# Transposing x, B and C by DMA while loading, in a kernel of two sequence mixers (convolution and complex state space)

## The chip, the cores and the metric

The kernel runs on one core of one Trainium2 chip. The metric is the device time of one execution in microseconds (us).

## The reference

The inputs are bf16 with sequence length S = 2048 and width D = 1024. Two independent halves are computed and laid side by side in the output of 1 x 2048 x 2048.

Half A: a causal convolution of length 4 on k, a product with v, a causal long convolution by a filter of length S, and a gate by q.

```python
k_shift = sum(k_pad[:, t:t + S, :] * shift_k[:, ks - 1 - t] for t in range(4))
kv = k_shift * v
y = irfft(rfft(kv, 2*S) * rfft(ssm_k, 2*S))[:S] + kv * ssm_D
a = q * y
```

Half B: a diagonal complex recurrence with 1024 states.

```python
Lam_bar = exp(dt * Lam)
B_bar = ((Lam_bar - 1.0) / Lam)[:, None] * (B_re + 1j * B_im)
Bu = einsum("bld,pd->blp", x, B_bar)
h[t] = Lam_bar * h[t-1] + Bu[t]
b = 2.0 * einsum("blp,dp->bld", h, C_re + 1j * C_im).real + x * Dskip
```

## The kernel before

Everything is emitted into one function, `full_kernel`; a framework then gives each engine its own instruction queue. It may move an instruction that has its inputs ready ahead of earlier ones that have not, and puts in the waits. The engines are TensorE (PE, its weight loads shown as PEld), VectorE (DVE), ScalarE (ACT), GpSimd (POOL) and SyncE (SP). Loads from device memory are issued on SP's queue by `dma` (L84), stores and some moves on POOL's by `dmas_` (L87). Each queue is in order.

Half B cuts time into 16 chunks of 128 steps (index i) and the states into 8 groups of 128 (index j). TensorE contracts over partitions, so it needs x, B and C with the contracted dimension on partitions, that is transposed from how they lie in memory.

- `b_load_x` (L248) loads a chunk of x of 128 x 1024 into `xn` (three buffers). `b_xT` (L253) transposes it by eight 128 x 128 TensorE transposes against `ident` into a PSUM tile `pt` and copies that to `xT` (seven buffers), on ACT, for chunk 0 on DVE.
- `bt_prep` (L596) does the same for the 16 blocks of B (j = 0..7, real and imaginary), through `bn` (three buffers) into `BT`; the real blocks are copied by DVE, the imaginary by ACT.
- `ct_load` (L609) and `ct_prep` (L614) do the same for the 16 blocks of C, through `bn` into `CT`, copied by ACT. The imaginary blocks are multiplied by -1 in that copy.
- `b_u` (L265) multiplies `BT` with `xT`, eight matmuls of 128 x 128 for each (i, j, c), and ACT copies the result to `u` (five buffers).
- `b_rot_ops` (L283) is the recurrence on DVE: 14 steps a chunk. It rotates `u` by the tables `ci` and `si`, runs two scans of 128 x 1024, and multiplies by the tables `eor` and `eoi` to give `h`.
- `b_y` (L337) multiplies `h` with `CT`, adds the skip term (`xT` with the diagonal matrices `Dd`), and the result goes out as `yo`.
- `gen_tables_a` and `gen_tables_b` (L216, L229) make the tables in the setup, on DVE and ACT. Their scratch arrays `sc_*` lie in the memory of `CT`, so `CT` can be written only when the tables are done. `params_rest` (L163) makes the small coefficients for them.

Half A is a Fourier transform split in two steps. Stage A1 makes 16 rows of kv on DVE from `krow` (six buffers) and `vt` (three buffers), eight ops each (`a1_kv_ops`, L397). It transforms them and the filter by matmuls (L427, L474) and stores them to device memory (`Ys_kv`, `Ys_h`). Stage A2 has 32 groups: load `l2k`, `l2h` and weights, matmuls (L508), a swap of the partition halves of `ha` into `hb` by DMA, two products on DVE (L519, L521), matmuls (L532, L533), store to `Vs`. Stage A3 has 16 rows: load `vv` and `qt`, matmuls, a product, store.

The order is written by hand as ticks: `at(t, kind, fn)` puts a step at tick t, and the main loop runs the ticks, with each tick's TensorE steps of A and B interleaved, then its DVE steps. Chunk i of the recurrence takes ticks 8i to 8i+7 and its `b_y` the eight after. `b_u` runs ahead at a rate of 1.5 groups a tick to tick 40 and 0.7 after, as far as the `u` buffers allow (`u_tick`). The part that concerns the change:

```python
tu = u_tick[(i, 0)]
at(tu - 12, "misc", lambda i=i: b_load_x(i))
at(tu - 2, "pe_b", lambda i=i: b_xT(i))
...
at(n // 2 - 1, "misc", lambda c=c, dd=dd: ct_load(c, dd))
at(n // 2, "pe_b", lambda c=c, dd=dd: ct_prep(c, dd, "s"))
```

Before the ticks a setup runs: x of chunk 0, `gen_tables_a`, the 16 `bt_prep` with `b_u` of chunk 0 one group behind them, `params_rest`, `gen_tables_b`, and the first loads of half A.

Of the kernel before, what the change touches and what calls it, by code (L numbers as in the profile page):

```python
# [13 lines left out]
ALU = mybir.AluOpType  # L14
F32 = mybir.dt.float32
BF16 = mybir.dt.bfloat16
# [45 lines left out]
def full_kernel(ctx, tc, A_q, A_k, A_v, A_shift_k, A_ssm_k, A_ssm_D, B_x, B_Lre, B_Lim, B_Bre, B_Bim,  # L62
                B_Cre, B_Cim, B_log_dt, B_Dskip, out, cfg=None):
    cfg = dict(cfg or {})
    nc = tc.nc
    P = 128
    S, D = A_q.shape[-2], A_q.shape[-1]
    L = S
    NP = B_Lre.shape[0]
    NJ = NP // P  # L70
    ND = D // P
    T = 128
# [5 lines left out]
    q, k, v, x = A_q[0], A_k[0], A_v[0], B_x[0]  # L78
# [5 lines left out]
    def dma(out_, in_):  # L84
        return nc.sync.dma_start(out_, in_)
# [6 lines left out]
    ps_t = ctx.enter_context(tc.tile_pool(name="ps_t", bufs=2, space=PSUM))  # L92
# [136 lines left out]
    def gen_tables_b():  # L229
        nc.vector.tensor_copy(ci[:], sc_vc)  # L230
        nc.vector.tensor_copy(si[:], sc_vs)
        for j in range(NJ):
            nc.scalar.activation(sc_rn[:, j, :], sc_vc[:, j, :], ACT.Copy, scale=br2[:, j:j + 1])
            nc.scalar.activation(sc_ang[:, j, :], sc_vs[:, j, :], ACT.Copy, scale=br2[:, j:j + 1])
        for j in range(NJ):
            nc.vector.scalar_tensor_tensor(eor[:, j, :], sc_vs[:, j, :], nbi2[:, j:j + 1], sc_rn[:, j, :], ALU.mult, ALU.add)
            nc.vector.scalar_tensor_tensor(eoi[:, j, :], sc_vc[:, j, :], bi2[:, j:j + 1], sc_ang[:, j, :], ALU.mult, ALU.add)
# [6 lines left out]
    state = {}  # L244
# [1 line left out]
    XT_BUFS = U_BUFS + 2  # L246

    def b_load_x(i):  # L248
        xn = xpool.tile([P, D], BF16, name="xn", bufs=3)
        dma(xn[:], x[i * T:(i + 1) * T, :])  # L250
        state[("xn", i)] = xn

    def b_xT(i, eng="s"):  # L253
        xn = state.pop(("xn", i))
        xT = xpool.tile([P, ND, T], BF16, name="xT", bufs=XT_BUFS)
        state[("xT", i)] = xT
        pt = ps_t.tile([P, ND, P], BF16, name="pt")
        for dd in range(ND):
            nc.tensor.transpose(pt[:, dd, :], xn[:, dd * P:(dd + 1) * P], ident[:])
        if eng == "v":  # L260
            nc.vector.tensor_copy(xT[:], pt[:])
        else:
            nc.scalar.copy(xT[:], pt[:])  # L263

    def b_u(i, j, c):  # L265
        xT = state[("xT", i)]
# [16 lines left out]
    def b_rot_ops(i):  # L283
        ops = []
# [304 lines left out]
        for o in ops:  # L589
            o()  # L590

    bnpool = ctx.enter_context(tc.tile_pool(name="bn", bufs=1))
    Bv = (B_Bre.rearrange("(j i) d -> i j d", i=P), B_Bim.rearrange("(j i) d -> i j d", i=P))
    Cv = (B_Cre, B_Cim)

    def bt_prep(j, c, eng):  # L596
        bn = bnpool.tile([P, D], BF16, name="bn", bufs=3)
        dma(bn[:], Bv[c][:, j, :])
        pt = ps_t.tile([P, ND, P], BF16, name="pt")
        for dd in range(ND):  # L600
            nc.tensor.transpose(pt[:, dd, :], bn[:, dd * P:(dd + 1) * P], ident[:])  # L601
        if eng == "v":
            nc.vector.tensor_copy(BT[:, j, c, :, :], pt[:])
        else:
            nc.scalar.copy(BT[:, j, c, :, :], pt[:])

    cnat = {}

    def ct_load(c, dd):  # L609
        cn_ = bnpool.tile([P, NP], BF16, name="bn", bufs=3)  # L610
        dma(cn_[:], Cv[c][dd * P:(dd + 1) * P, :])
        cnat[(c, dd)] = cn_

    def ct_prep(c, dd, eng):  # L614
        cn_ = cnat.pop((c, dd))
        pt = ps_t.tile([P, NJ, P], BF16, name="pt")
        for j in range(NJ):
            nc.tensor.transpose(pt[:, j, :], cn_[:, j * P:(j + 1) * P], ident[:])
        dst = CT[:, :, c, dd * P:(dd + 1) * P]
        if c == 0:  # L620
            if eng == "v":
                nc.vector.tensor_copy(dst, pt[:])
            else:
                nc.scalar.copy(dst, pt[:])
        else:
            if eng == "v":
                nc.vector.tensor_scalar(dst, pt[:], -1.0, None, ALU.mult)
            else:
                nc.scalar.mul(dst, pt[:], -1.0)

    NT = 8 * (NCH + 1) + 8
    ev = {}
# [34 lines left out]
    if DO_B:  # L667
        for i in range(NCH):
            t0 = 8 * i
            rops = {}  # L670
            at(t0, "misc", lambda i=i, rops=rops: rops.update({"l": b_rot_ops(i)}))
            for kk, sl in enumerate([[0, 1], [2, 3], [4, 5], [6], [7], [8, 9], [10, 11], [12, 13]]):
                for oi in sl:
                    at(t0 + kk, "dve_b", lambda oi=oi, rops=rops: rops["l"][oi]())
            for kk in range(8):
                at(t0 + 8 + kk, "pe_b", lambda i=i, kk=kk: b_y(i, kk // 4, kk % 4))
            if i >= U_PRO:
                tu = u_tick[(i, 0)]
# [74 lines left out]
    if DO_B:  # L753
        for i in range(U_PRO):
            b_load_x(i)
        gen_tables_a()
        b_xT(0, "v")
        for j in range(NJ):
            bt_prep(j, 0, "v")
            bt_prep(j, 1, "s")  # L760
            if j >= 1:
                b_u(0, j - 1, 0)
                b_u(0, j - 1, 1)
            if j == 1:
                params_rest()
        b_u(0, NJ - 1, 0)
        b_u(0, NJ - 1, 1)
        for i in range(1, U_PRO):
            b_xT(i)
            for j in range(NJ):  # L770
                for c in range(2):
                    b_u(i, j, c)
# [72 lines left out]
```

## Time and profile before

| what | value |
|---|---|
| median of 3 runs | 431.73 us (428.91 to 433.8) |
| profiled execution, first to last instruction | 431.1 us; the page gives no time outside it |
| PE busy | 380.7 us, 88% of the span |
| DVE busy | 350.7 us, 81% |
| ACT busy | 303.6 us, 70% |
| POOL busy | 130.2 us, 30% |
| SP's DMA queue | 58.60 MB, 42.7% of 16 engines' span |
| POOL's DMA queue | 43.01 MB, 28.8% |
| mean granted TensorE clock | 0.974 |

Matmuls are pipelined and their records overlap, so a busy PE is not PE at its peak, and the shares are averages over stages with different limits. In the slices each digit is the busy share of a fortieth of the span in tenths. In the groups a row is one source line on one engine, with its count, its busy time, the mean duration of one, and the idle time of the engine just before with what ended it. In the chain each step goes back to what released it.

### The profile page before, as it was taken

Reading aid. Unit: us, or ns where it says so; the run is one execution under the profiler, and the core shown is the slowest. Engines: PE = TensorE matmul, PEld = TensorE weight load, DVE = VectorE, ACT = ScalarE, POOL = GpSimd, SP = SyncE. Lnnn points to the kernel's source line nnn. Section 1 sums busy time; section 2 is a strip of 40 time slices with the busy share of each in tenths; the row PEclk is TensorE's granted clock in tenths of the full one; section 3 lists DMA queues with packets and bytes.
Section 4 is the critical chain, followed back from the end, with each engine's and each line's share of the span. In section 5 each row is a group of like instructions: output and inputs, shape, how many; then the busy total and the mean of one; then the engine's idle time right before and its main releaser. Section 6 shows DMA issues by size and latency. Waiting matters only on the chain.

```text
span 431.1 us, 9757 instructions
## 1 busy us (share of the span) xinstructions
PE 380.7 (88%) x3713; PEld 259.7 (60%) x3713; DVE 350.7 (81%) x642; ACT 303.6 (70%) x531; POOL 130.2 (30%) x224
## 2 busy tenths in 40 slices
PE   2589799797987997999899999999899999997784
PEld 2578687575765875775556566566465666763331
DVE  2989999999999999936897979797959637976830
ACT  1977999787886887646678877878568783344451
POOL 4000344464654455311222232322122211012121
PEclk9979999999999899999999999999899999999989
DMA  7879987778776544397778687879666523959981
GB/s 247 285 255 309 336 289 254 265 240 249 276 235 205 167 163 159 120 334 238 229 241 263 217 247 245 265 234 295 195 217 181 165 69 135 298 176 396 403 316 73
DMA packets 41353, 102.23 MB, mean 237 GB/s; under 512 B 6621, under 2 KB 8925, under 8 KB 41306
## 3 DMA queue, kind: packets, MB, share of 16 engines
q1 hardware_dynamic: 27322, 58.60, 42.7%
q0 software_dynamic: 13984, 43.01, 28.8%
q8 instruction: 29, 0.48, 0.5%
q14 instruction: 18, 0.15, 0.1%
HBM read 59.64 MB, written 33.55 MB: 216 GB/s over the span
## 4 chain that ended last, share of the span: by engine, by line
PE 42%; DVE 28%; issue 12%; DMA 10%; ACT 5%; POOL 2%; SPq 0%; POOLq 0%; DVEq 0%; ACTq 0%
PE pu L274 13%; PE py L345 13%; DVE m L409 5%; PE psa L508 5%; DVE acc L410 4%; DMA hb<-ha 3%; PE psa L533 3%; PE psa L532 3%; DVE ta L305 2%; DVE tb L308 2%; DVE acc L414 2%; DMA out_dram<-ot 2%; POOL out_dram L88 2%; DMA bn<-in_B_C_re_dram 1%; PE pt L601 1%
## 5 line engine op out<-in xcount | busy, mean ns | idle before, releaser
L274 PE MATMUL pu<-xT,BT 128*128 128x128 bf16 x2048 | 156.1, 222 | 0.5 <-ACT xT L263 0.3
L274 PEld LDWEIGHTS <-BT 128*128 128x128 bf16 x2048 | 136.2, 100 | 33.5 <-issue 2.4
L345 PE MATMUL py<-CT,h 128*128 128x512 bf16 x512 | 140.2, 382 | 2.3 <-ACT yo L355 2.3
L345 PEld LDWEIGHTS <-h 128*128 128x128 bf16 x512 | 46.7, 98 | 45.5 <-issue 4.9
L88 POOL DMA_DIRECT2D hb<-ha x64 | 33.4, 526 | 88.9 <-ACT ha L509 85.0
L534 ACT CAST vsb<-psa 128x512 bf16<-128x512 f32 x64 | 37.0, 602 | 25.7 <-PE psa L533 24.8
L88 POOL DMA_DIRECT2D Ys_h<-ysbh x64 | 45.6, 716 | 30.8 <-ACT ysbh L475 29.4
L277 ACT CAST u<-pu 128x512 bf16<-128x512 f32 x64 | 39.4, 615 | 13.2 <-PE pu L274 13.1
L428 ACT CAST ysb<-psa 128x512 bf16<-128x512 f32 x64 | 38.5, 644 | 13.7 <-PE psa L427 13.3
L519 DVE TENSOR_TENSOR ha<-x,ha 128x1024 bf16<-128x1024 bf16 x32 | 21.9, 684 | 27.8 <-DMA hb<-ha 18.7
L475 ACT CAST ysbh<-psa 128x512 bf16<-128x512 f32 x64 | 38.7, 641 | 5.5 <-issue 2.3
L509 ACT CAST ha<-psa 128x512 bf16<-128x512 f32 x64 | 36.8, 598 | 7.3 <-PE psa L508 6.3
L509 ACT CAST x<-psa 128x512 bf16<-128x512 f32 x64 | 36.9, 593 | 7.3 <-PE psa L508 5.2
L308 DVE TENSOR_TENSOR_SCAN tb<-rtab,tb 128x1024 bf16<-128x1024 f32 x16 | 36.6, 2285 | 0.0
L305 DVE TENSOR_TENSOR_SCAN ta<-rtab,ta 128x1024 bf16<-128x1024 f32 x16 | 36.5, 2280 | 0.0
L427 PE MATMUL psa<-acc,F1t 128*128 128x512 bf16 x64 | 24.6, 392 | 12.0 <-DVE acc L414 11.9
L564 ACT CAST ot<-psa 128x512 bf16<-128x512 f32 x32 | 17.9, 589 | 24.4 <-DMA out_dram<-ot 14.8
L409 DVE TENSOR_TENSOR m<-krow,wbc 128x1024 bf16<-128x1024 bf16 x48 | 32.4, 675 | 0.0
L410 DVE TENSOR_TENSOR acc<-acc,m 128x1024 bf16<-128x1024 bf16 x48 | 32.3, 673 | 0.0
L532 PE MATMUL psa<-ha,wts 128*128 128x512 bf16 x64 | 24.5, 384 | 4.2 <-DVE ha L519 4.0
L88 POOL DMA_DIRECT2D Ys_kv<-ysb x32 | 17.8, 557 | 33.9 <-ACT ysb L428 33.9
L350 PE MATMUL py<-Dd,xT 128*128 128x128 bf16 x128 | 28.0, 219 | 0.0
(139 smaller groups left out, 628.5 us busy)
## 6 DMA issues: line engine op xcount, KB each, us to landing
Ys_kv<-ysb POOLq DMA_DIRECT2D x32, 256.0 KB, 2.9
Ys_h<-ysbh POOLq DMA_DIRECT2D x64, 128.0 KB, 3.3
l2k<-Ys_kv SPq DMA_DIRECT2D x16, 512.0 KB, 6.0
l2h<-Ys_h SPq DMA_DIRECT2D x16, 512.0 KB, 4.2
hb<-ha POOLq DMA_DIRECT2D x64, 128.0 KB, 3.7
Vs<-vsb POOLq DMA_DIRECT2D x16, 512.0 KB, 5.9
vv<-Vs SPq DMA_DIRECT2D x32, 256.0 KB, 6.6
xn<-in_B_x_dram SPq DMA_DIRECT2D x16, 256.0 KB, 4.3
```

The lines of the kernel that those rows point to most:

```text
L88: return nc.gpsimd.dma_start(out_, in_)
L274: nc.tensor.matmul(pu[:, c, jl, :], BT[:, j, c, dd, :], xT[:, dd, :], start=(dd == 0), stop=(dd == ND - 1))
L277: nc.scalar.copy(u[:, :, j - 1:j + 1, :], pu[:])
L305: ops.append(lambda: nc.vector.tensor_tensor_scan(fl(st["ta"]), fl(rtab), fl(st["ta"]), 0.0, ALU.mult, ALU.add))
L308: nc.vector.tensor_tensor_scan(fl(st["tb"]), fl(rtab), fl(st["tb"]), 0.0, ALU.mult, ALU.add)
L345: nc.tensor.matmul(py[:], h[:, c, j, :], CT[:, j, c, dh * 512:(dh + 1) * 512], start=(j == 0 and c == 0), stop=(j == NJ - 1 and c == 1))
L409: ops.append(lambda jj=jj: nc.vector.tensor_mul(st["m"][:], krows[n2 - jj][:], wbc[:, jj, :]))
L410: ops.append(lambda: nc.vector.tensor_add(st["acc"][:], st["acc"][:], st["m"][:]))
L428: nc.scalar.copy(ysb[:, dh * 512:(dh + 1) * 512], pt[:])
L475: nc.scalar.copy(ysbh[:, :, n2l, :], pt[:].rearrange("p (c d) -> p c d", c=2))
L509: nc.scalar.copy(d_[:, dh * 512:(dh + 1) * 512], pt[:])
L532: nc.tensor.matmul(pt[:], wts[:, gi, 1, :], ha[:, dh * 512:(dh + 1) * 512], start=True, stop=False)
```

## The change

x, B and C are transposed by the DMA itself, by `dma_start_transpose` on SP's queue, straight from device memory into `xT`, `BT` and `CT`. The TensorE transposes, the PSUM tiles and the copies of these three go, and with them `xn` and `bn`. The transposes of the filter in half A (`a1h_T`) stay. A chunk of x and a block of B is one DMA of 128 x 1024; C is four DMAs of 512 x 1024. The 16 loads of B are emitted ahead of `gen_tables_a`, the four of C after `gen_tables_b`.

[...]the -1 of C's imaginary part moves: `eoi` is made with the opposite sign, the step that used it for the real part of `h` changes from subtract to add, and the one for the imaginary part from add to subtract, so that the imaginary part of `h` comes out negated.

```diff
         for j in range(NJ):
             nc.vector.scalar_tensor_tensor(eor[:, j, :], sc_vs[:, j, :], nbi2[:, j:j + 1], sc_rn[:, j, :], ALU.mult, ALU.add)
-            nc.vector.scalar_tensor_tensor(eoi[:, j, :], sc_vc[:, j, :], bi2[:, j:j + 1], sc_ang[:, j, :], ALU.mult, ALU.add)
+            nc.vector.scalar_tensor_tensor(eoi[:, j, :], sc_vc[:, j, :], nbi2[:, j:j + 1], sc_ang[:, j, :], ALU.mult, ALU.subtract)
...
     def b_load_x(i):
-        xn = xpool.tile([P, D], BF16, name="xn", bufs=3)
-        dma(xn[:], x[i * T:(i + 1) * T, :])
-        state[("xn", i)] = xn
-
-    def b_xT(i, eng="s"):
-        xn = state.pop(("xn", i))
         xT = xpool.tile([P, ND, T], BF16, name="xT", bufs=XT_BUFS)
+        nc.sync.dma_start_transpose(xT[:], x[i * T:(i + 1) * T, :])
         state[("xT", i)] = xT
-        pt = ps_t.tile([P, ND, P], BF16, name="pt")
-        for dd in range(ND):
-            nc.tensor.transpose(pt[:, dd, :], xn[:, dd * P:(dd + 1) * P], ident[:])
...
-        ops.append(lambda: nc.vector.tensor_sub(st["h"][:, 0, :, :], st["h"][:, 0, :, :], st["u"][:, 1, :, :]))
+        ops.append(lambda: nc.vector.tensor_add(st["h"][:, 0, :, :], st["h"][:, 0, :, :], st["u"][:, 1, :, :]))
...
-            nc.vector.tensor_add(st["h"][:, 1, :, :], st["h"][:, 1, :, :], st["u"][:, 1, :, :])
+            nc.vector.tensor_sub(st["h"][:, 1, :, :], st["h"][:, 1, :, :], st["u"][:, 1, :, :])
...
-    def bt_prep(j, c, eng):
...
-    def ct_prep(c, dd, eng):
...
+    def bt_load(j, c):
+        nc.sync.dma_start_transpose(BT[:, j, c, :, :], Bv[c][:, j, :])
+
+    def ct_load(c, hf):
+        nc.sync.dma_start_transpose(CT[:, :, c, hf * 512:(hf + 1) * 512], Cv[c][hf * 512:(hf + 1) * 512, :])
...
                 at(tu - 12, "misc", lambda i=i: b_load_x(i))
-                at(tu - 2, "pe_b", lambda i=i: b_xT(i))
...
-        for n, (c, dd) in enumerate([(c, dd) for dd in range(ND) for c in range(2)]):
-            at(n // 2 - 1, "misc", lambda c=c, dd=dd: ct_load(c, dd))
-            at(n // 2, "pe_b", lambda c=c, dd=dd: ct_prep(c, dd, "s"))
...
         for i in range(U_PRO):
             b_load_x(i)
+        for j in range(NJ):
+            for c in range(2):
+                bt_load(j, c)
         gen_tables_a()
-        b_xT(0, "v")
         for j in range(NJ):
-            bt_prep(j, 0, "v")
-            bt_prep(j, 1, "s")
-            if j >= 1:
-                b_u(0, j - 1, 0)
-                b_u(0, j - 1, 1)
-            if j == 1:
+            b_u(0, j, 0)
+            b_u(0, j, 1)
+            if j == 0:
                 params_rest()
...
         gen_tables_b()
+        for hf in range(2):
+            for c in range(2):
+                ct_load(c, hf)
```

More of the change, by code (lines that the diff above doesn't have):

```diff
@@ L248, in b_load_x @@
     def b_load_x(i):
-        xn = xpool.tile([P, D], BF16, name="xn", bufs=3)
-        dma(xn[:], x[i * T:(i + 1) * T, :])
-        state[("xn", i)] = xn
-    def b_xT(i, eng="s"):
-        xn = state.pop(("xn", i))
         xT = xpool.tile([P, ND, T], BF16, name="xT", bufs=XT_BUFS)
+        nc.sync.dma_start_transpose(xT[:], x[i * T:(i + 1) * T, :])
         state[("xT", i)] = xT
-        pt = ps_t.tile([P, ND, P], BF16, name="pt")
-        for dd in range(ND):
[L259 to L263, printed above, removed]
     def b_u(i, j, c):
@@ L590, in run @@
             o()
-    bnpool = ctx.enter_context(tc.tile_pool(name="bn", bufs=1))
     Bv = (B_Bre.rearrange("(j i) d -> i j d", i=P), B_Bim.rearrange("(j i) d -> i j d", i=P))
     Cv = (B_Cre, B_Cim)
-    def bt_prep(j, c, eng):
[L597 to L612, printed above, removed]
-    def ct_prep(c, dd, eng):
[L615 to L629, printed above, removed]
+    def bt_load(j, c):
+        nc.sync.dma_start_transpose(BT[:, j, c, :, :], Bv[c][:, j, :])
+    def ct_load(c, hf):
+        nc.sync.dma_start_transpose(CT[:, :, c, hf * 512:(hf + 1) * 512], Cv[c][hf * 512:(hf + 1) * 512, :])
     NT = 8 * (NCH + 1) + 8
@@ L755, in full_kernel @@
             b_load_x(i)
+        for j in range(NJ):
+            for c in range(2):
+                bt_load(j, c)
         gen_tables_a()
-        b_xT(0, "v")
         for j in range(NJ):
-            bt_prep(j, 0, "v")
-            bt_prep(j, 1, "s")
-            if j >= 1:
-                b_u(0, j - 1, 0)
-                b_u(0, j - 1, 1)
-            if j == 1:
-                params_rest()
[L766 to L772, printed above, removed]
+            b_u(0, j, 0)
+            b_u(0, j, 1)
+            if j == 0:
+                params_rest()
         gen_tables_b()
+        for hf in range(2):
+            for c in range(2):
+                ct_load(c, hf)
     if DO_A:
```

## Prediction

> **What bounds the kernel now.** I read the page's slices first, then the table by windows, the timeline where the setup ends, and the chain of work that ended last. The slices (each digit a tenth of 10.8 us) show that the bound changes:
>
> ```profile
> PE   2589799797987997999899999999899999997784
> ...
> DVE  2989999999999999936897979797959637976830
> ...
> PEclk9979999999999899999999999999899999999989
> DMA  7879987778776544397778687879666523959981
> ```
>
> VectorE (DVE) is full from slice 2 to slice 16, TensorE (PE) from slice 17 to slice 35, and at the end neither is. The windows put sizes to it (window, length, then busy us of PE, weight loads, DVE, ACT, POOL, granted clock, DMA share, GB/s):
>
> ```profile
> 36.00:48.00 12.00, 10.13 (x159) 8.93 (x157) 11.96 (x18) 10.15 (x15) 1.08 (x2) 1.00 0.98 342
> 60.00:80.00 20.00, 19.37 (x228) 15.09 (x226) 20.00 (x36) 20.00 (x33) 9.81 (x15) 1.00 0.84 274
> 240.00:280.00 40.00, 39.65 (x331) 23.81 (x330) 34.72 (x61) 32.25 (x60) 11.96 (x23) 1.00 0.79 254
> 320.00:360.00 40.00, 39.89 (x358) 25.04 (x356) 24.80 (x42) 30.40 (x56) 10.70 (x20) 1.00 0.49 148
> 385.00:432.00 47.00, 33.25 (x171) 14.78 (x169) 21.16 (x30) 17.14 (x32) 9.77 (x18) 0.94 0.77 292
> ```
>
> Three stages. From 11 to 172 us DVE sets the pace: 11.96 of 12 and 20.00 of 20 us, with PE waiting on its products. From about 178 to 385 us PE does: 39.65 and 39.89 of 40 us. After 385 us the last section waits on vv loads, ACT copies and output stores; the change has nothing there. The last column but one is the warning: between 36 and 80 us the DMA engines are already 84 to 98% busy.
>
> The seam between setup and stage one, on DVE (start, length):
>
> ```profile
> 32.19 0.69 DVE L406 TENSOR_TENSOR acc<-krow,wbc 128x1024 bf16<-128x1024 bf16 x1
> ...
> 33.92 0.68 DVE L603 COPY BT<-pt 128x1024 bf16<-128x1024 bf16 x1
> 34.52 0.34 DVE L237 SCALAR_TENSOR_TENSOR eoi<-CT,bi 128x128 bf16<-128x128 f32 x1
> ...
> 37.31 0.68 DVE L292 TENSOR_TENSOR ta<-u,ci 128x1024 bf16<-128x1024 bf16 x1
> ```
>
> Here the convolution's first product starts at 32.19, the last BT copy on DVE is at 33.92, the last table op ends at 34.8, and the first rotation op (L292) at 37.31 follows ACT's last BT copy (34.58) and the last u copy (36.31). Two convolution ops of 0.6 us lie before 34.8, so setup holds DVE until an effective 33.6 us.
>
> **What is removed, as the groups price it** (busy, mean ns | idle before):
>
> ```profile
> L263 ACT COPY xT<-pt 128x1024 bf16<-128x1024 bf16 x15 | 15.9, 1060 | 1.7 <-PE pt L259 1.7
> ...
> L601 PE MATMUL pt<-ident,bn 128*128 128x128 bf16 x128 | 12.4, 258 | 6.4 <-ACT BT L605 3.6 <-DMA bn<-in_B_B_im_dram 1.9 <-DVE BT L603 0.6
> ...
> L603 DVE COPY BT<-pt 128x1024 bf16<-128x1024 bf16 x8 | 5.5, 687 | 2.1 <-PE pt L601 2.0
> ```
>
> Records of pipelined matmuls overlap, so 219 ns is not the price. On the chain eight transposes count 0.45 us, that is 56 ns each:
>
> ```profile
> 262.81 0.45 PE pt L259 x8
> ```
>
> **What the Trainium skill says.** "DMA: Bandwidth & Descriptors", section "Latency and other measured facts", gives a DMA transpose 261 GB/s with a non-contiguous middle dimension and 350 to 400 when contiguous. The trace before has no transposing DMA. Its plain loads on the same SP queue moved 12.98 MB in 82.2% of 48 us (the DMA view of 12 to 60 us), that is 329 GB/s or 0.80 us of all 16 engines per 256 KB. "Advanced Engine Details and Errata", "X-Bar Transpose (TRN2)", says that they are as fast as regular DMAs; nothing here shows that either. "DMA: Bandwidth & Descriptors", "Bandwidth", lists for earlier generations 262,144 cycles for 8,192 tiles SBUF to SBUF, 32 cycles a tile. "TensorE: Matmul & The Clock Gate", Part 4, gives about 275 ns for one TensorE transpose in a kernel; the trace's record is 219 ns and its share of the chain 56.
>
> **The transposing DMA's price, from both sides.** The cheap end is the plain load's 0.80 us per 256 KB. At 261 GB/s it is 262,144 B / 261 GB/s = 1.0 us. The dear end is an estimate from the skill's 32 cycles: with a tile of 16 rows by 128 columns (that page's "Constraints") and SyncE's 1.2 GHz ("Trainium Kernel Development and Optimization", "NeuronCore Architecture"), 64 tiles x 32 cycles make 1.7 us, during which SP may issue nothing else. I take d = 1.0 us, because the page calls it measured, and keep 0.8 and 1.7. SP's plain issue took 0.33 to 0.43 us, so at d = 1.0 the transposes and not their issue set the pace.
>
> **Part 1, BT and xT of the setup.** Gone: 17 x 8 TensorE transposes, 8 ACT copies of 1.0 us, and 9 DVE copies that follow each other at about 0.6 us. On DVE that is 9 x 0.6 = 5.4 us, plus 2.0 us that DVE sat idle in front of them (L603's row: 2.1). Added on SP: 17 transposes with nothing to wait for, right after the parameter loads, which end at 3.1 us. The loads of k, v and ssm_k that slipped in between bn loads at 5.27 us (bn has three buffers) now stand behind all 17. Nothing but SP's issue waits for that: the queue's readers are DVE's convolution and PE's ssm_k transposes.
> - BT complete: 3.1 + 17d + 2.5 (landing; the shortest xn took 2.6) = 22.6 us at d = 1.0. The rotation starts 1.7 us later, as it did after ACT's last BT copy: 24.3, or in general 7.3 + 17d.
> - k rows: seven issues of 0.45 and 4.3 us to land: 3.1 + 17 + 3.1 + 4.3 = 27.5 us.
> - DVE is free of tables at 33.6 - 5.4 - 2.0 = 26.2 us.
> So DVE starts its stage at 26.2 instead of 33.6 at best, a gain of 7.4. The loads of A_shift_k, 1 MB on POOL's queue, share the engines in the same microseconds (3.2 us by 1 MB / 329 GB/s), and some of that falls on the transposes. I count a gain of 5.0 us. At d = 1.7 the start is 36.2, a loss of 2.6.
>
> **Part 2, CT.** 16 x 8 transposes and 16 ACT copies (8.9 + 9.1 us) go; they lay between 37 and 74 us, beside a full DVE, so they were hidden: 0. Added: four transposes of 1 MB, 4 us each at d = 1.0, which wait for the tables (they share memory with CT) at the head of SP's in-order queue. Behind them stand k and v rows for later steps; six k buffers and three v buffers cover about three convolution steps, some 25 us at one step every 8.5. CT's first reader, b_y(0), started at 63.6 us, and CT would be in by about 50. Price 0; if the cover is gone, each late k row stops DVE.
>
> **Part 3, x.** Seven of the fifteen later xT copies came before 168 us beside the full DVE: 0. Eight came in PE's stage, from 182 us. The chain holds five of them, 5 x 0.45 = 2.3, and one ACT xT wait of 0.92: 3.2 us gained. If all eight count it is 3.6. With xn gone a load takes one of seven xT buffers directly and waits for b_y(i-7); by the ticks that buffer is free at least two ticks ahead, so it stops no queue.
>
> **Part 4, the sign.** eoi, L326 and L331 change add to subtract on the same shapes (683 and 682 ns): 0.
>
> **What it costs.** 48 transposes x (1.0 - 0.80) = 10 us of DMA time. Some 32 fall before 60 us, 6.4 us more where 11% of 48 us was free: just full. Later ones meet the hb<-ha swaps, for which DVE waited 18.7 us in all. I take 1.5 us lost, between 0 and 4.
>
> **Sum.** 431.1 - 5.0 - 3.2 + 1.5 = 424.4 us for the profiled span. The page gives no time outside the span; the runs' median of 431.73 is 0.6 above it. So 425.0 us.
>
> **Rivals.**
> - Better: the DMA takes all of it, 431.7 - 7.4 - 3.6 = 420.7, or less when PE, rid of 24 transposes in stage one, also has less left at 178 to 190 us before the first L508 (perhaps 2): 418.7. For it: the chain there is PE. Against: at 188 us the l2k load lands, and that ends the wait anyway.
> - No change: k rows come late behind 17 transposes, so DVE idles until 33.6, and only 3.2 - 1.5 is left: 431.7 - 1.7 = 430.0. For it: the queue is in order. Against: the rotation's 14 ops can fill DVE meanwhile.
> - Slower, one mechanism: crossbar transposes do not share the DMA engines well, and d grows under traffic. Place: SP's queue from 3 to 80 us. The start 7.3 + 17d overtakes 33.6 by as much as PE gains (3.2 - 1.5) at d = 1.65; that is the turning point. At d = 2.0 it starts at 41.3, 7.7 late. CT takes 16 x (2.0 - 0.8) = 19 us more of full DMA; about half of it reaches DVE through late k rows or PE through b_y(0): 9. Less 3.2: 431.7 + 7.7 + 9 - 3.2 = 445. For it: 84 to 98% DMA share at just that place, and no trace of such a DMA. Against: the skill's 261 GB/s.
> - That it does nothing it says: excluded by the diff, since the PE transposes are deleted.
>
> **How the numbers follow.** Forecast near 425: 0.46; better, near 420: 0.08; no change, near 430: 0.16; slower: 0.30, with its tail to 445 and beyond. About 1%, 4.3 us, is what a measurement can tell from no change, since the three runs spread by 1.1%. Faster by over 1% takes the first two, less a little of the forecast's edge: 0.53; within 1%: 0.17; slower: 0.30. The likeliest case alone spans 420 to 429; the range to leave out 2 in 10 goes from 416 to 444.
>
> **What would show it.** Right: DVE starts L292 or L406 at 25 to 29 us and the convolution's last L414 (171.3 before) comes some 5 us earlier; PE's stage is 3 us shorter; transposes of xT and BT follow each other on SP at 1.0 to 1.2 us. Wrong: SP gaps of 1.6 us or more between them, DVE waits on DMA krow, vt or BT in the first 80 us, or PE waiting on CT before b_y(0). A loss that sits after 200 us, at hb or l2k, would make the DMA cost the mis-sized term.

## The result and the profile after

The changed kernel takes 446.16 us (median of 3 runs, 445.11 to 446.55), against 431.73 before: a ratio of 1.032 (95% interval 1.025 to 1.039). It is slower by 14 us, where 425.0 was forecast, and 2 us beyond the range. The profiled execution spans 444.7 us against 431.1. The slices of the page after (a digit is now a tenth of 11.1 us):

```profile
PE   0760194889979889799889989999979999998674
...
DVE  0949935889999999996688797988985946995830
...
PEclk9995587899989999989999999999999999999999
DMA  7999999887876745439877888888967433759981
```

Counting from 0: before, DVE was full from slice 2 to 16. Now it has holes in slice 2 (a 4) and in slices 5 and 6 (3 and 5) and is not full again before slice 9, PE is almost idle in slices 3 and 4, and the DMA row stands at 9 from slice 1 to 6. The windows (length, then busy us of PE, weight loads, DVE, ACT, POOL, granted clock, DMA share, GB/s; the share adds up the packets' times, and in the traces below it passes 1):

```profile
36.00:48.00 12.00, 1.44 (x4) 0.38 (x4) 12.00 (x19) 1.07 (x2) 0.57 (x1) 0.50 1.04 241
60.00:80.00 20.00, 13.44 (x171) 11.43 (x169) 11.53 (x19) 10.86 (x20) 7.19 (x12) 0.83 1.13 266
...
240.00:280.00 40.00, 38.09 (x326) 23.18 (x325) 34.30 (x61) 29.84 (x56) 11.41 (x22) 1.00 0.82 251
320.00:360.00 40.00, 37.18 (x309) 22.31 (x308) 32.31 (x56) 29.35 (x55) 11.12 (x21) 1.00 0.61 193
385.00:432.00 47.00, 39.14 (x280) 20.81 (x279) 33.65 (x52) 20.92 (x39) 9.20 (x17) 1.00 0.91 339
```

From 36 to 48 us the DMA engines moved 342 GB/s at a share of 0.98 before; now they are as busy and move 241. From 60 to 80 us DVE fell from 20.00 to 11.53 us. Four landmarks place the loss: the convolution's last product with vt goes from 171.2 to 188.1 (16.9 late), the first matmul on l2h from 190.4 to 206.3 (15.9 late), the last matmul on hb from 361.8 to 376.3 (14.5 late), the end 13.6 late. All of it arises before 188 us, and PE's stage gives a little back. The first landmark, before and after:

```profile
171.24 0.67 DVE L414 TENSOR_TENSOR acc<-acc,vt 128x1024 bf16<-128x1024 bf16 x1
```
```profile
188.10 0.68 DVE L402 TENSOR_TENSOR acc<-acc,vt 128x1024 bf16<-128x1024 bf16 x1
```

Up to it DVE was busy for 159.1 us before (6.2 of it the copies that are now gone) and for 153.7 after: the same work, and 34.4 us of idle time in place of 12.2. The seam on DVE (start, length):

```profile
32.64 0.69 DVE L394 TENSOR_TENSOR acc<-krow,wbc 128x1024 bf16<-128x1024 bf16 x1 [1.52 <-DMA krow<-in_A_k_dram]
...
35.88 0.34 DVE L237 SCALAR_TENSOR_TENSOR eoi<-CT,nbi 128x128 bf16<-128x128 f32 x1
36.14 0.68 DVE L280 TENSOR_TENSOR ta<-u,ci 128x1024 bf16<-128x1024 bf16 x1
```

The first convolution product moved by 0.4 us only, and the first rotation op (L280 here) is even 1.2 us earlier than before, though far from the 24.3 that was forecast. SP's queue (start, length of the issue) shows why, and what stands behind it; the last line is of the kernel before:

```profile
3.14 1.36 SPq L250 DMA_TRANSPOSE xT<-in_B_x_dram  x1
4.55 2.79 SPq L584 DMA_TRANSPOSE BT<-in_B_B_re_dram  x1
7.39 1.31 SPq L584 DMA_TRANSPOSE BT<-in_B_B_im_dram  x1
8.74 1.31 SPq L584 DMA_TRANSPOSE BT<-in_B_B_re_dram  x1
...
28.67 3.27 SPq L85 DMA_DIRECT2D krow<-in_A_k_dram  x7
...
36.25 3.87 SPq L587 DMA_TRANSPOSE CT<-in_B_C_re_dram  x1
...
54.29 4.56 SPq L250 DMA_TRANSPOSE xT<-in_B_x_dram  x3
58.90 0.58 SPq L85 DMA_DIRECT2D krow<-in_A_k_dram  x1
```
```profile
31.62 0.42 SPq L85 DMA_DIRECT2D krow<-in_A_k_dram  x1
```

A transpose holds SP for 1.31 us and the next starts 1.35 us after it: 256 KB in 1.35 us is 194 GB/s. The 17 of the setup end at 28.63, and the first seven k row loads follow. C's four then hold SP from 36.25 to 53.6, with a filter half and three x chunks behind them, and only at 58.90 the first k row for a later step goes out; before it went at 31.62. Where DVE's hole at 60 to 80 us comes from is in the chain (start, length):

```profile
65.48 9.75 DMA Ys_h<-ysbh
...
77.88 5.83 DMA Ys_h<-ysbh
...
87.83 6.58 DMA Ys_h<-ysbh
```

Stores on POOL's queue, whose median landing over the whole kernel is 3.0 us, take 6 to 10 us here. Their buffer holds ACT, ACT holds the PSUM tiles, and PE's products and then DVE's convolution wait. The packet counts are the last clue; the first line is of before, the second of after:

```profile
DMA packets 41353, 102.23 MB, mean 237 GB/s; under 512 B 6621, under 2 KB 8925, under 8 KB 41306
```
```profile
DMA packets 84741, 102.18 MB, mean 230 GB/s; under 512 B 56157, under 2 KB 58461, under 8 KB 84698
```

The same bytes go in twice the packets: some 50,000 under 512 B are new.

Some executions of the kernels below ran longer than the rest: the ratios leave them out, the medians do not, the landmarks of x alone and of C late come from such executions and are rough, and the kernel with 512-byte pieces was profiled a second time for that reason.

### The profile page after: what moved, and what is told of

It is laid out like the page before. It is cut to its first block, busy times and chain, and to the rows that moved or that the text cites. A ratio compares the mean times of both kernels' runs of the same rounds, so it can differ in the third digit from the quotient of the medians.

```text
span 444.7 us, 8904 instructions
## 1 busy us (share of the span) xinstructions
PE 364.9 (82%) x3329; PEld 239.3 (54%) x3329; DVE 346.9 (78%) x633; ACT 267.3 (60%) x492; POOL 129.8 (29%) x224
## 2 busy tenths in 40 slices
DMA packets 84741, 102.18 MB, mean 230 GB/s; under 512 B 56157, under 2 KB 58461, under 8 KB 84698
## 3 DMA queue, kind: packets, MB, share of 16 engines
q0 software_dynamic: 13984, 43.01, 28.5%
## 4 chain that ended last, share of the span: by engine, by line
PE 30%; DVE 30%; DMA 15%; issue 12%; SPq 7%; POOL 3%; ACT 2%; POOLq 0%; DVEq 0%; ACTq 0%
PE py L333 11%; PE pu L262 9%; SPq L584 5%; DMA Ys_h<-ysbh 5%; DMA hb<-ha 5%; DVE m L397 5%; DVE acc L398 4%; PE psa L496 3%; DVE ta L293 3%; PE psa L521 2%; DVE tb L296 2%; PE psa L520 2%; DMA out_dram<-ot 2%; DVE acc L402 2%; POOL out_dram L88 2%
## 5 line engine op out<-in xcount | busy, mean ns | idle before, releaser
L262 PE MATMUL pu<-xT,BT 128*128 128x128 bf16 x2048 | 157.8, 226 | 15.4 <-DMA BT<-in_B_B_re_dram 13.8
L262 PEld LDWEIGHTS <-BT 128*128 128x128 bf16 x2048 | 137.6, 101 | 55.4 <-DMA BT<-in_B_B_re_dram 15.4
L333 PE MATMUL py<-CT,h 128*128 128x512 bf16 x512 | 142.3, 383 | 11.7 <-DVE h L314 8.6
L416 ACT CAST ysb<-psa 128x512 bf16<-128x512 f32 x64 | 36.3, 612 | 29.6 <-PE psa L415 28.6
L463 ACT CAST ysbh<-psa 128x512 bf16<-128x512 f32 x64 | 36.0, 620 | 13.3 <-DMA Ys_h<-ysbh 12.4
L507 DVE TENSOR_TENSOR ha<-x,ha 128x1024 bf16<-128x1024 bf16 x32 | 21.9, 683 | 27.2 <-DMA hb<-ha 14.1
L520 PE MATMUL psa<-ha,wts 128*128 128x512 bf16 x64 | 24.3, 380 | 6.7 <-DVE ha L507 6.7
```

Of the source, the lines that this page charges most:

```text
L262: nc.tensor.matmul(pu[:, c, jl, :], BT[:, j, c, dd, :], xT[:, dd, :], start=(dd == 0), stop=(dd == ND - 1))
L333: nc.tensor.matmul(py[:], h[:, c, j, :], CT[:, j, c, dh * 512:(dh + 1) * 512], start=(j == 0 and c == 0), stop=(j == NJ - 1 and c == 1))
L416: nc.scalar.copy(ysb[:, dh * 512:(dh + 1) * 512], pt[:])
L463: nc.scalar.copy(ysbh[:, :, n2l, :], pt[:].rearrange("p (c d) -> p c d", c=2))
```

## The experiments

"Last kv" below is the start of the convolution's last product with vt: 171.2 before, 188.1 after. "PE's stage" is the time from there to the last matmul on hb: 190.6 before, 188.2 after.

### One operand at a time, and no crossbar at all

The kernel before with one operand's part of the change: x only, B only, C only (with the sign).

> Only x is transposed by the DMA; B and C go through TensorE as before. Theory 1 (order of the queue: a transposing DMA costs by holding SP's in-order queue in front of loads that VectorE needs): sixteen transposes of 1.3 us spread over 300 us hold back little, TensorE loses 8 transposes in its own stage, so 428 to 431 us against 431.7 before. Theory 2 (crossbar transposes take more of the DMA engines wherever they run, and slow what runs beside them): 433 us or more, with longer waits on the hb swaps. Theory 3 (the order on TensorE's queue in the setup) expects no change in the setup: the parameter transpose at 7.3 us.

> Only B is transposed by the DMA; x and C go through TensorE as before. Theory 1: the first k rows come behind the transposes of B, some 29 us, about when they were first used before (32 us), and nothing stands in front of later loads: 429 to 434 us. Theory 2: 16 transposes at 1.35 instead of 0.8 us cost 9 us of DMA time at the start: 435 to 440 us. Theory 3: if matmuls that wait for B are put ahead of the parameter transpose on TensorE, VectorE starts its tables at 11 us instead of 7.5, 4 us more.

> Only C is transposed by the DMA, in four DMAs right after the tables, with the sign in the table; x and B go through TensorE as before. Theory 1: this is where most of the loss is, since four DMAs of 4.0 to 4.6 us hold SP for 17 us in front of k, v, ssm_k and x: 437 to 444 us, with VectorE idle some 8 to 15 us between 50 and 80 us. Theory 2: 16 x 0.25 to 0.3 us more DMA time than plain loads, 4 to 5 us at most: 432 to 436 us.

The change with every transpose turned into a plain load of the same bytes in the same places, for instance:

```diff
-        nc.sync.dma_start_transpose(BT[:, j, c, :, :], Bv[c][:, j, :])
+        nc.sync.dma_start(BT[:, j, c, :, :].rearrange("p a t -> p (a t)"), Bv[c][:, j, :])
```

> The changed kernel with each transposing DMA replaced by a plain DMA of the same bytes, same issuer and same place in the queue; the data land untransposed, so the output is not the reference's. Theories 1 and 2: without the crossbar's price the recast setup gains what the prediction counted for it, 421 to 427 us. Theory 3, or any loss by the new order alone (late k rows behind B and C): 433 us or more, because the order of SP's queue is that of the changed kernel.

| kernel | median us | ratio to before, 95% | last kv |
|---|---|---|---|
| x only | 435.85 | 1.005 (1.001 to 1.009) | 175.4 |
| B only | 437.55 | 1.016 (1.008 to 1.023) | 174.3 |
| C only | 426.51 | 0.990 (0.982 to 0.998) | 166.3 |
| all plain | 423.50 | 0.983 (0.975 to 0.990) | 166.2 |

All plain settles the first question: with the change's order of issues on SP and everything that it removes, but without the crossbar, as the path of a transposing DMA is called here, the kernel is 1.7% faster than before. Its last kv:

```profile
166.20 0.68 DVE L402 TENSOR_TENSOR acc<-acc,vt 128x1024 bf16<-128x1024 bf16 x1
```

The loss is in the transposing form, 188.1 - 166.2 = 21.9 us at the last kv. DVE did the same work up to there (153.0 us, and 153.7 in the change), so it is waiting. B alone and, by its ratio, x alone took the time that theory 2 gave them (435 to 440; 433 or more). C alone was forecast at 432 us or more by both theories; it is 1% faster than before instead, and beats both kernels. Its four transposes hold SP 4.80 to 6.18 us each, among plain loads and stores, but the first seven k row loads had gone out between 5 and 19 us in the gaps between B's loads, two more with their v rows at 31 to 33 us, and DVE was full from 36 to 60 us (11.94 of 12 and 12.00 of 12). Its 4.9 us at the last kv are no gain in waiting: up to there DVE did four pairs of scans where the kernel before did five, 153.3 us of work instead of 159.1, and was idle for 13.1 us instead of 12.2. That work comes later, in PE's stage, which is still 4.9 us shorter (185.7). Why is not shown.

### Is it the order of the queues?

First, PE: in the change's queue the matmuls of chunk 0, waiting for BT, stand ahead of the parameter transpose (11.1 us, 7.3 before). Second, SP: C stands ahead of k, v and the filter. Four kernels: the matmuls behind the transpose (`with tc.issue_after(praw_T.ins):` around the two `b_u`); C's loads at tick 3, behind the first k, v, x and filter loads; both; and both with half A's first loads ahead of B's. The second edit:

```diff
+        for hf in range(2):
+            for c in range(2):
+                at(3, "ct", lambda c=c, hf=hf: ct_load(c, hf))
...
-        for hf in range(2):
-            for c in range(2):
-                ct_load(c, hf)
```

> The changed kernel with one order edge more: on TensorE's queue the matmuls of chunk 0 stand behind the transpose of the parameters. Theory 3 (TensorE's order): VectorE starts the tables at 7.5 instead of 11.3 us, and 3 to 4 us come back: 441 to 443 us against 446. Theory 1 (SP's queue: transposes of B, then of C, ahead of what the convolution and the next chunks of x need): the tables are early but the k rows still come at 32 us and C, which waits for the tables, only moves up by up to 4 us, so between 442 and 446 us.

> The changed kernel with the four transposes of C emitted at tick 3 instead of straight after the tables, so that on SP's queue they stand behind x of chunk 1, the k and v rows to step 3 and the second half of the filter; all transposes stay. Theory 1: the hole of VectorE between 55 and 80 us goes, the last kv product (188.1 us in the changed kernel) comes at 173 to 178, and the run takes 431 to 436 us. Theory 2 (the crossbar's bandwidth, wherever it is put): the bytes are the same, so 441 us or more.

> Both edits together: C late, and the parameter transpose first on TensorE. Theory 1 with theory 3 as a second, smaller part: 428 to 434 us, 2 to 4 better than C late alone. If the two parts hide each other (the k rows at 32 us then set the start), the same as C late alone.

> As the run with both edits, and the first loads of half A (k rows, v, filter) are emitted ahead of the 16 transposes of B, so that they go out among the first ones. Theory 1: the first convolution product starts at 27 to 28 us, as soon as the tables are done, instead of 32, while B is 4 to 5 us later; 425 to 430 us, better than before. Theory 2: no better than with both edits, since the DMA engines are full in the first 30 us either way.

PE's order: 446.97 us, 1.032 (1.027 to 1.038), last kv 188.4; the rotation starts at 32.9 and nothing comes of it. C late: 449.14 (441.4 to 450.5, no ratio), last kv 188.2. Both: 453.08, 1.044 (1.035 to 1.053), last kv 189.8. Half A first: 445.97, 1.029 (1.023 to 1.035), last kv 183.0 (with 5.9 us less work of DVE before it than in the change), although the first convolution product now comes at 19.9 us. Theory 3's 3 to 4 us did not come back, and the other three kernels stayed far from the 436 us or less that theory 1 gave them. Order alone is not the cause. The store landings of C late, between 48 and 60 us (the DMA view: KB each, median us from issue to landing), show what C meets when it is issued later:

```profile
Ys_h<-ysbh POOLq DMA_DIRECT2D x4, 128.0 KB, 14.2
```

### Which operand's crossbar costs how much?

The change with one operand plain and the two others by crossbar.

> The changed kernel with B's 16 loads as plain DMAs of the same tiles and bytes in the same places of SP's queue (B lands untransposed, so the output is not the reference's); x and C stay with the crossbar. All three plain gave 423.5 us and a last kv product (acc<-acc,vt) at 166.2; all three transposing 446.2 and 188.1, a price of 22 us. Theory A (each transposing byte costs its longer time on full DMA engines, wherever it lies): B holds 4 of the 9 MB that are transposed before 90 us, so 22 x 4/9 = 10 us come back: last kv product near 178, time near 436. Theory B (the price is made where CT's and x's transposes meet plain loads and output stores, between 34 and 80 us; what B's do is to push the k, v and filter loads into that place): SP is through B's loads by about 15 us, the rows for the first steps are in when CT is issued, and most comes back: last kv product near 170, time near 428, as in the kernel with C alone (426.5).

> The changed kernel with C's four loads as plain DMAs of the same bytes in the same places (C lands untransposed, so the output is not the reference's); B and x stay. Theory A: C holds 4 of 9 MB, so 10 us come back: last kv product near 178, time near 436. Theory B: the transposes that meet the stores are then x's alone (1 to 1.3 MB of 5.3), so most of the 22 us comes back but for what B's transposes cost in the first 30 us (B alone cost 3 to 6 us): last kv product near 173, time near 431. SP's holds between 36 and 54 us fall from 4 to 5 us each to under 2, and Ys_h stores land in 3 to 5 us.

> The changed kernel with x's loads as plain DMAs (x lands untransposed, so the output is not the reference's); B and C stay with the crossbar. Theory A: x holds about 1 of 9 MB before 90 us, so 2 to 3 us come back: last kv product near 185, time near 443. Theory B: CT still meets loads and stores at 36 to 54 us, x's transposes at 54 to 77 us no longer hold SP for 4.4 to 5.9 us each while Ys_h stores wait: about 5 us come back: last kv product near 183, time near 441. If x's transposes among the stores were the main cause, over 12 us would come back: time under 434.

| plain | median us | ratio to before, 95% | last kv | PE's stage |
|---|---|---|---|---|
| B | 438.25 | 1.009 (1.004 to 1.013) | 177.0 | 187.5 |
| C | 439.96 | 1.013 (1.008 to 1.019) | 181.7 | 187.1 |
| x | 438.70 | 1.012 (1.005 to 1.019) | 183.0 | 183.6 |
| all | 423.50 | 0.983 (0.975 to 0.990) | 166.2 | 184.4 |

The kernel before was slower on that chip (434.1), so the ratios count. At the last kv, above the 166.2 of all plain, x with C costs 10.8, x with B 15.5, B with C 16.8. Solving the three, B costs 10.8, C 6.1 and x 4.8; the sum, 21.6, is the 21.9 of all three. (Each landmark is one execution, on different chips, so these are good to 1 or 2 us; DVE's work up to it is 153.0 to 153.7 us in all five.) Theory B, a price made in one place, between 34 and 80 us, falls: it had the last kv near 170 and 173 for B and C plain, and 177.0 and 181.7 came. The prices add. B's is what theory A gave it (178), C's is smaller than its share of the bytes (178 expected, 181.7 measured); for x, theory B's 183 came and not theory A's 185. x pays twice: 4.8 us before 188, and 3.5 us or so in PE's stage, which is 187.1 to 188.2 wherever x goes by crossbar and 183.6 to 184.4 where it is plain. There its six transposes, the first of which held SP for 4.96 us at 203.08, lie beside the hb<-ha swaps of POOL's queue. That the swaps carry the loss is not shown: they land in 3.8 us in the median with x by crossbar, with x plain and with all plain.

### The transfers by themselves

> The disputed cost by itself; the kernel leaves out the whole computation. Stretches, each begun when the one before has landed: (1) 16 transposes of 128x1024 alone; (2) the same with 16 stores of 256 KB on POOL's queue; (3) 16 transposes, each behind a plain load of 256 KB on SP's queue; (4) both; (5) 16 plain loads and 16 stores, no transpose; (6) four transposes of 512x1024 alone; (7) four of these with 16 stores. Theory A (a fixed longer time a byte): 1.35 us each in (1), that is 194 GB/s; (2) and (3) are the sum, 16 x (1.35 + 0.80) = 34 us; (4) 16 x 2.95 = 47 us; (5) 16 x 1.6 = 26 us. Theory B (mixing lowers the rate further): (2), (3) and (4) run at 170 to 200 GB/s in all, so (2) and (3) take 42 to 49 us, (4) 63 to 74, while (5) keeps over 300 GB/s; stores in (2) and (4) land in over 10 us. If (2) equals the sum and (3) does not, SP's hold and not the stores is what costs.

In this first form the stores of its fourth stretch ran in its third, so only its first two are used: 1.35 us for each transpose alone, and 188 GB/s at a share of 1.21 for transposes among stores, with holds of 4 to 7 us at SP and stores landing in 12.5 us. It was written again, with each stretch held until everything before had landed.

> Transfers by themselves; the kernel leaves out the whole computation. Nine stretches, each begun when everything before it has landed: 16 stores of 256 KB on POOL's queue (S); 16 plain loads of 256 KB on SP's (L); 16 such loads in 256-byte pieces (P); 16 transposes of 128x1024 (T); T with S; P with S; L with S; L and T alternating on SP; all three. From the runs so far T alone is 16 x 1.35 = 21.6 us and L alone 16 x 0.66 = 10.6; S alone I put at 10.6 to 12.8. If only a fixed longer time a byte is paid, T with S takes the sum, 32 to 34 us, L with T 32 us, all three 43 to 45. If the stores are slowed by the crossbar beyond it, T with S takes 40 to 44 us and L with S stays at its sum, 21 to 24 us. If the small packets are what costs, P alone takes about 21 us like T, and P with S as long as T with S; if the crossbar is, P alone takes 11 to 14 us.

The windows of the second form, one execution (length, busy us of DVE and POOL, clock, DMA share, GB/s), in this order: S, L, P, T, T with S, P with S, L with S, L with T, all three:

```profile
36.00:50.30 14.30, 0.01 (x1) 8.65 (x16) 1.00 0.82 293
67.80:82.00 14.20, 0.20 (x3) 0.00 (x0) 1.00 0.84 295
99.30:120.40 21.10, 0.27 (x3) 0.00 (x0) 1.00 1.19 199
137.60:162.10 24.50, 0.27 (x3) 0.00 (x0) 1.00 0.93 171
179.40:224.40 45.00, 0.29 (x3) 8.55 (x16) 1.00 1.06 186
241.90:272.30 30.40, 0.26 (x2) 8.56 (x16) 1.00 1.02 276
289.80:313.40 23.60, 0.25 (x2) 8.56 (x16) 1.00 0.94 356
330.80:366.20 35.40, 0.27 (x2) 0.00 (x0) 1.00 1.06 237
383.50:428.30 44.80, 0.19 (x2) 8.55 (x16) 1.00 1.07 281
```

Each window has 3 us or so of first landing in it (T: 24.5 against 16 x 1.35 = 21.6), so a sum of two windows counts it twice. Three readings. The same 4.2 MB take 14.2 us as plain loads, 21.1 in 256-byte pieces and 24.5 through the crossbar: of the crossbar's 10.3 us more, 6.9 are the pieces. Plain loads and stores together take less than their sum (23.6 us against 28.5), and so do pieces with stores (30.4 against 35.4) and plain loads with transposes on one queue (35.4 against 38.7); crossbar and stores take more (45.0 against 38.8), where it was expected that pieces with stores would take as long if packets were all. The stores themselves (the DMA view: KB each, median us from issue to landing; alone, beside the crossbar, beside the pieces, beside plain loads):

```profile
out_dram<-s POOLq DMA_DIRECT2D x16, 256.0 KB, 4.3
```
```profile
out_dram<-s POOLq DMA_DIRECT2D x16, 256.0 KB, 12.9
```
```profile
out_dram<-s POOLq DMA_DIRECT2D x16, 256.0 KB, 6.7
```
```profile
out_dram<-s POOLq DMA_DIRECT2D x16, 256.0 KB, 8.0
```

So two things hold at once: a price of the transfer itself, two thirds of it packet size, and a mutual slowing with POOL's stores beyond the sum, which, of the three kinds of load, only the crossbar brings. Stores land later beside any load, but latest beside the crossbar.

### The packets in the kernel

Plain loads in pieces of 256 B in the place of every transpose; the same with C late; and pieces of 512 B.

```diff
-        nc.sync.dma_start_transpose(BT[:, j, c, :, :], Bv[c][:, j, :])
+        nc.sync.dma_start(BT[:, j, c, :, :], (B_Bre, B_Bim)[c][j * P:(j + 1) * P, :].rearrange("(b r) (a e) -> (r a) b e", b=8, a=8))
```

> The changed kernel with every transposing DMA replaced by plain loads of the same bytes in pieces of 256 B (1,024 packets for 128x1024; C in 16 DMAs of 256 KB instead of four of 1 MB), in the same places of SP's queue. The operands land in another order, so the output is not the reference's. If the small packets are the price, this runs like the change: first rotation op near 36, last kv product near 188, time near 446. If the crossbar is the price (its own rate, and SP held at the issue), it runs like the plain loads: rotation near 24, last kv product near 166, time near 424. In between (near 435): both hold a part, to be read from the share of the engines at 12 to 24 us (1.0 at 192 GB/s with the crossbar, 352 GB/s plain).

> Plain loads in pieces of 256 B in the place of every transpose, with C's loads issued behind the first k, v and filter loads, in the order that the crossbar was run in (449.1 us, last kv product 188.2). The operands land in another order, so the output is not the reference's. If the packets are the price: last kv product 184 to 188, time 440 to 446 (about 4 us less than with the crossbar, which holds SP 1.35 instead of 1.15 us and costs some 3.7 us in PE's stage). If the order made the loss in the other run with pieces: last kv product 170 to 175, time near 430.

> The same in pieces of 512 B, twice as long and half as many (512 packets for 128x1024), in the order of the change. The operands land in another order, so the output is not the reference's. If the time goes with the number of packets whatever their size, half of the price of 22 us is left: last kv product near 177, time near 434. If it goes with bytes once a packet is 512 B or longer: near the plain loads, rotation near 24, last kv product 166 to 169, time 423 to 427.

> The kernel with 512-byte pieces again (its output is not the reference's, as the operands land in another order). It took 0.989 of the kernel before, the plain loads 0.983 and the change 1.032. If a packet of 512 B moves at nearly the plain rate, BT's loads follow each other on SP at 0.85 us, the first rotation op is near 26 and the last kv product at 168 to 171 (plain: 23.8 and 166.2).

| loads | packets | median us | ratio to before, 95% | first rotation op | last kv | PE's stage |
|---|---|---|---|---|---|---|
| plain | 43,205 | 423.50 | 0.983 (0.975 to 0.990) | 23.8 | 166.2 | 184.4 |
| 512 B | 59,653 | 426.56 | 0.989 (0.985 to 0.993) | 26.2 | 172.6 | 184.1 |
| 256 B | 84,358 | 441.80 | 1.022 (1.014 to 1.030) | 31.1 | 186.5 | 184.5 |
| 256 B, C late | 84,357 | 433.90 | 1.004 (1.000 to 1.008) | 31.6 | 180.7 | 183.8 |
| crossbar | 84,741 | 446.16 | 1.032 (1.025 to 1.039) | 36.1 | 188.1 | 188.2 |

The window from 12 to 24 us, where B's loads run, for plain, 512 B, 256 B and crossbar:

```profile
12.00:24.00 12.00, 7.23 (x103) 5.68 (x101) 11.93 (x49) 11.33 (x20) 0.00 (x0) 0.93 1.03 352
```
```profile
12.00:24.00 12.00, 9.14 (x107) 7.43 (x105) 11.50 (x50) 9.53 (x13) 0.00 (x0) 1.00 1.16 288
```
```profile
12.00:24.00 12.00, 10.01 (x80) 7.38 (x78) 11.84 (x51) 10.48 (x23) 0.00 (x0) 1.00 1.39 218
```
```profile
12.00:24.00 12.00, 8.95 (x72) 6.57 (x70) 11.31 (x47) 7.73 (x9) 0.00 (x0) 1.00 0.99 192
```

At shares of about 1 and more the engines move 352, 288, 218 and 192 GB/s. In pieces of 256 B, B's loads follow each other on SP at 1.19 us, in 512 B at 0.88, plain at 0.68, against 1.35 for the crossbar: SP is held with no crossbar at all, and here, where the order is the same in all four, the pieces make three quarters of what a transpose costs over a plain load.

Small packets alone slow the kernel, then: 1.022 and 1.004 in two orders, where plain loads have 0.983. Their share of the change's loss is not shown, for two reasons. First, with pieces in the change's places, C's go out ahead of the k rows, which the change does not do (k rows at 28.67, C at 36.25):

```profile
25.89 4.32 SPq L588 DMA_DIRECT2D CT<-in_B_C_re_dram  x4
...
44.43 3.85 SPq L85 DMA_DIRECT2D krow<-in_A_k_dram  x7
```

The first convolution product then starts at 49.83 instead of 32.64, so the 186.5 - 166.2 = 20.3 us of this run are not the packets' time alone. Second, with C late (last kv 180.7 where 184 to 188 was put for "packets are the price", so a miss), DVE does more before the last kv: six pairs of scans, not five.

| loads | last kv | DVE busy to it | DVE idle |
|---|---|---|---|
| plain | 166.2 | 153.0 | 13.2 |
| 512 B | 172.6 | 153.3 | 19.3 |
| 256 B | 186.5 | 154.6 | 31.9 |
| 256 B, C late | 180.7 | 164.8 | 15.8 |
| crossbar | 188.1 | 153.7 | 34.4 |
| crossbar, C late | 188.2 | 150.3 | 37.8 |

Of the 14.5 us by which its last kv is late, only 2.6 are idle time. In the whole time, by the ratios, the packets cost 2.1 to 3.9 of the 4.9 points between all plain and the change. The crossbar's own part, its lower rate and its slowing of the stores, was not separated; with C late, the Ys_h stores between 48 and 60 us land in 14.2 us beside the crossbar and in 4.9 beside pieces. With 512 B, where the work of DVE is the same, 6.4 of the 21.9 us remain, a little more than expected (172.6 where 168 to 171 was put), and the kernel is faster than before: the price does not go with the packets' number alone.

## Why the prediction was wrong, point by point

- **The stages and the bound**: right for the kernel before. DVE set the pace to the last kv, and the loss arises there, as waiting of DVE. The DMA share of 84 to 98%, called the warning, was the right place to look.
- **d, the step that failed.** It was taken at 1.0 us because the skill's page "DMA: Bandwidth & Descriptors", section "Latency and other measured facts", has 261 GB/s as measured. Here it is 1.35 us, 194 GB/s, for x and B, in the setup as alone, and 0.97 to 1.15 for C's longer transposes by SP's holds; "as fast as regular DMAs" ("Advanced Engine Details and Errata", "X-Bar Transpose (TRN2)") is not borne out either. Nor is the plain load 0.80: 16 of them alone took 10.3 us less than 16 transposes, so a transpose costs not 0.2 us more than a plain load but 0.65, and the 10 us of DMA time for 48 transposes should have been up to 31. Before 60 us the prediction had 6.4 us more where 5.3 (11% of 48) were free, "just full". At 0.65 its 32 transposes need 21 us there, an estimate that is 15 us or so too many; 16.9 us were lost by the last kv. The dear end, 1.7, was too dear. (The 32 cycles a tile behind it stand on the page under "Why a DMA increments its semaphore by 16 and not by 1", not under "Bandwidth", as time in the sequencer without the transfer.) "DMA: Bandwidth & Descriptors" holds a hint to the true size: its "Specifications" ask for at least 512 B per transfer for line rate. The windows above agree below that size (218 GB/s at 256 B, 352 for plain loads), while at 512 B it was still 288. But no view of before could show that the crossbar's packets are under 512 B.
- **Part 1, the rotation at 7.3 + 17d**: the formula gives 30.3 at 1.35, and 36.1 was measured; the 256-byte pieces at 1.19 give 27.5 and 31.1 was measured. The base of 7.3 was short by 4 to 6 us. Of the 5.8, 3.2 lie in the parameter transpose behind the waiting matmuls, which the prediction did not see coming: with that order changed the rotation starts at 32.9. The other 2.6 are about what SP's two long holds in the setup add (2.79 and 2.27 us in place of 1.31). DVE, meant to gain 5 us here, was busy 6.07 of 12 us from 24 to 36.
- **Part 2, price 0**: wrong for the cost of the transposes: C's cost 6.1 us at the last kv. The sentence "if the cover is gone, each late k row stops DVE" named a small part of it: k rows for later steps left at 58.90, and DVE waited on them for 2.9 us. The chain runs through the store landings, which the prediction did not price; they held ACT and PE to 95 us.
- **Part 3, x in PE's stage**: near in sum, and partly by luck. It gained 190.6 - 188.2 = 2.4 us; 3.2 less 1.5 was forecast. Without the crossbar it is 6.2, and x by crossbar takes 3.7 back: both terms were too small by 2 to 3 us, which cancels.
- **Part 4, the sign**: nothing, as forecast; L314 and L319 take 682 and 685 ns, the steps before took 682 and 683.
- **The sum without d**: all plain took 8 us off where the sum took 6.7, so the removals were not priced too high in sum, and the mis-sized term is the transpose's.
- **The rivals**: the slower one had the sign, the place (SP's queue from 3 to 80 us) and the size (445), from terms that were partly wrong: the start was not 7.7 late but 1.2 early, and the turning point of d = 1.65 was too high, since at 1.35 the kernel already lost. It held the start of the rotation for the measure, while the work behind it decides. Its reason, that d grows under traffic, holds beside POOL's stores (45.0 us against 38.8), not beside plain loads (35.4 against 38.7), and d is 1.35 in a quiet queue already.
- **What would show it**: of the signs of "wrong", SP's gaps stayed at 1.35 us but for two in the setup (2.8 and 2.3) and x chunks under traffic (4.4 and 5.9), DVE waited on krow for 2.9 us only, and PE's waits on CT did not come. The waits that came were on BT and on Ys_h stores. One sign misled: a loss after 200 us was to mean that the DMA cost was the mis-sized term. The loss sits before 188 us, and the DMA cost is that term all the same.

## What to carry to other kernels

Price a transposing DMA by its packets: here some 1,024 of 256 B for 128 x 1024 bf16 (49,536 new ones under 512 B for 48 tiles), 194 GB/s on 16 engines and SP held for as long, about 0.65 us of all engines dearer than a plain load of 256 KB. Where the DMA engines were at 84 to 98% already, that price came back as waiting of the engine that sets the pace, and it was more than the removed TensorE and ACT work was worth. What stands behind the transposes on SP counts too: C alone, issued when the k rows for the next steps were out, lost nothing (426.5 us, the best version here that keeps the output), though the engines were no less full there (a share of 1.22 from 36 to 48 us).

Look at the packets under 512 B in the page before trusting a share of busy time: about 1.0 meant 352 GB/s in one kernel and 192 in another. And before two kernels are compared at a landmark, see whether the engine that sets the pace has done the same work by then: pieces with C late had done 12 us more than the others, and that, not waiting, made most of what they were late.

## What the runs showed of the hardware

- Crossbar transposes on SP's queue and stores on POOL's slow each other beyond the sum, 45.0 us against 38.8, and stores land in 12.9 us instead of 4.3. Pieces of 256 B do not do this (30.4 against 35.4, landing in 6.7), nor do plain loads (23.6 against 28.5, landing in 8.0).
- Adding 16 plain loads to transposes and stores cost nothing: 44.8 us against 45.0, and stores landed in 7.1 us. Why is open.
- C's transposes of 512 x 1024 in the change held SP for 3.87 to 4.59 us, less by the byte than the 1.35 us of 128 x 1024; with C late, among stores, for 5.71 to 11.39 us.
